# Seven-product down projection for a seventh unit, norms and statistics re-dealt between VectorE and ScalarE, weight sums packed, and a new order table

## The chip, the cores and the metric

The kernel runs on one core of one Trainium2 chip. The time is device microseconds of one launch; less is better. A run's time is that of its slowest core, which is here the only one.

## The reference, cut to what matters

All tensors are bf16. A sequence of 2048 tokens with 512 features goes through two layers; each layer is a long convolution block (A) and a gated feed-forward block (B), with a layer norm without weights ahead of each, and a residual add behind each:

```python
def _A_ref(q, k, v, shift_k, ssm_k, ssm_D):
    # k_shift: k convolved with 4 taps per feature
    kv = k_shift * v
    # y: causal convolution of kv with ssm_k, length 2048, by rfft of length 4096
    y = y + kv * ssm_D[None, None, :]
    return q * y

def _B_ref(x, w_gate, w_up, w_down):          # 512 x 1792, 512 x 1792, 1792 x 512
    g = _silu(x @ w_gate)
    u = x @ w_up
    return (g * u) @ w_down

x = A_q
x = x + _A_ref(_layernorm(x), A_k, A_v, A_shift_k, A_ssm_k, A_ssm_D)
x = x + _B_ref(_layernorm(x), B_w_gate, B_w_up, B_w_down)
# and the same two lines once more
```

The convolution's result y is the same in both layers (its inputs are k, v and the filters), so the kernel computes it once.

## The kernel before, in words

**Units.** The tokens are cut into four blocks c = 0..3 of 512, and each block into two halves h = 0, 1 of 256. The feed-forward of one half block in one layer is a *unit*, written (layer, c, h): 16 units. They run in the order (0,c,0), (0,c,1), (1,c,0), (1,c,1) for c = 0..3, overlapping at their edges. The convolution of block c is done by spectra (matrix products with sine and cosine tables, products of spectra on VectorE named `t`, `Z`, and an inverse) and runs between the units, up to about 200 us.

**A unit.** VectorE or ScalarE makes the statistics of the rows (`ln_stats`, L932: bn_stats and bn_aggr on VectorE; `ln_stats_act`, L943: sums and squared sums by ScalarE's accumulator), GpSimd makes `rstd` by a power (L923), then the norm `n` is applied by VectorE (`normalise`, L987) or by ScalarE (L982, after VectorE has made a small factor `nmr`, L973 or L976). `prologue` (L1002) multiplies n with y, adds it to the residual `xc`, takes statistics again and makes the second norm `z` in the same two ways. `z` is turned by two transposing DMAs on the SyncE queue (L1017) to `zT`, from which TensorE makes gate and up (L432), tile `pf`. ScalarE empties them (`sg` with silu, `hr` or `ht` as a copy), VectorE multiplies the two, and the down projection follows. For some groups of feature tiles the multiplied tile is first turned by DMAs (L1217, `sg<-hr`).

**Down projection, plain.** 14 feature tiles times two token tiles: 28 matmuls of 128x512 into two banks `pd` (L1298). ScalarE copies the two banks to `dn` (L1343, or L1346 where its accumulator also takes the row sums for the next norm's statistics), and one VectorE add puts them into `xc` (L1350).

**Down projection by seven products.** `seven` (L1078) treats the product as a 2x2 block product: seven block products instead of eight. VectorE makes three sums `cb` per group of feature tiles (L1087, L1089, L1091); five sums of `w_down` are made once (`weight_sums`, L1059). A unit then has 49 matmuls of 128x256 (L1108) into four banks. `add_seven` (L1112) has ScalarE empty four banks to `mt` (L1120) and VectorE add them to `xc` in five operations (L1125 to L1132). Before the change six units do this: (1,2,0), (1,2,1), (0,3,0), (0,3,1), (1,3,0) and, for half its features, (1,3,1).

**What sets the order.** Every operation is recorded in a plan with its engine, and the table `ORDER` gives each recorded operation its place. The instructions of every engine are then issued in that order; each engine takes them one after the other, SyncE its DMAs too. Tiles live in rings of slots (`h`, `k`, `hs`, `dg`, `s8`, ...); a new tile of a ring waits until the old one in its slot has been read. The tables at the top say for each unit which engine does what:

- `ST1`: units whose first statistics ScalarE makes; `ST2`: the same for the second.
- `N_ACT` and `Z_ACT`: units whose norm n and z ScalarE makes.
- `STRASSEN`: units whose down projection goes by seven products, with the number of groups.

Of the kernel before, what the change touches and what calls it, by code (L numbers as in the profile page):

```python
# [1616 lines left out]
```

## Time and profile before

| | |
|---|---|
| median of 3 runs | 338.16 us (337.48 to 338.86) |
| the profiled execution | 339.0 us |
| its span, first to last instruction | 337.2 us |
| TensorE busy | 331.3 us (98%), granted clock 0.999 |
| VectorE busy | 310.0 us (92%) |
| ScalarE busy | 268.4 us (80%) |
| GpSimd busy | 40.3 us (12%) |

The profile is of one execution; its span is 1.8 us shorter than that execution's time. Engines are called PE (TensorE matmul), PEld (its weight loads), DVE (VectorE), ACT (ScalarE), POOL (GpSimd) and SP (SyncE). A row of the timeline reads: start, duration, engine, line, operation, output and inputs, how many; in brackets the idle time before it and what ended that. Records of matmuls and of VectorE operations overlap a little with the next one, so the distance between two starts is what an operation occupies.

### The profile page before, as it was taken

The page shows a single profiled execution, that of the slowest core. Times are in us where ns is not written, and L with a number is a line of the kernel's source. Part 1 is how long each engine was busy: PE and PEld are TensorE (multiplying, and loading weights), DVE is VectorE, ACT ScalarE, POOL GpSimd, SP SyncE. Part 2 cuts the span into 40 slices and gives each one's busy share as a digit, 9 for nine tenths or more (in the row PEclk, how much of TensorE's full clock was granted, in tenths as well). Part 3 has the DMA queues.
Part 4 walks back from the last instruction along what each step waited for, and adds up shares of the span by engine and source line. Part 5 has one row for each costly group of instructions (what it writes and reads, how often), then busy time and mean ns, then how long its engine had stood idle before and what let it go on. Part 6 is the DMA issues. An engine that isn't in the chain of part 4 may idle for free.

```text
span 337.2 us, 6314 instructions
## 1 busy us (share of the span) xinstructions
PE 331.3 (98%) x2321; PEld 210.1 (62%) x2321; DVE 310.0 (92%) x580; ACT 268.4 (80%) x542; POOL 40.3 (12%) x54
## 2 busy tenths in 40 slices
PE   8999999999999999999999999999999999999996
PEld 7765864745344556654545465564656797879994
DVE  7799999997999999799899999999999887989785
ACT  7899999999987665899999883858576765658673
POOL 4000100031001010231100201034000000100000
PEclk9999999999999999999999999999999999999999
DMA  7999703476345467941533595747423320212001
GB/s 249 359 284 363 87 10 68 80 175 138 79 96 94 95 124 157 227 95 13 137 80 64 105 173 131 170 80 133 101 50 62 64 50 31 50 32 53 13 2 62
DMA packets 77449, 37.37 MB, mean 111 GB/s; under 512 B 67685, under 2 KB 73706, under 8 KB 77418
## 3 DMA queue, kind: packets, MB, share of 16 engines
q1 hardware_dynamic: 75632, 30.61, 39.6%
q0 software_dynamic: 1632, 6.29, 9.9%
q8 instruction: 18, 0.29, 0.4%
q14 instruction: 13, 0.11, 0.1%
q10 hardware_dynamic: 154, 0.07, 0.1%
HBM read 12.33 MB, written 2.10 MB: 43 GB/s over the span
## 4 chain that ended last, share of the span: by engine, by line
PE 74%; DVE 13%; DMA 7%; ACT 2%; issue 2%; SPq 1%; POOL 0%; DVEq 0%
PE pf L432 40%; PE pd L1298 13%; PE ps L1108 9%; PE ps L432 5%; PE pf L1182 4%; DVE t L774 3%; DMA Z<-t 3%; PE ps L580 2%; DMA kn<-in_A_k_dram 2%; DVE ka L730 1%; DMA kc<-ka 1%; DVE bst L937 1%; DVE hr L1215 1%; SPq L734 1%; DMA zT<-z 1%
## 5 line engine op out<-in xcount | busy, mean ns | idle before, releaser
L432 PEld LDWEIGHTS <-zT 128*128 128x128 bf16 x496 | 48.3, 98 | 55.9 <-DMA zT<-z 2.0
L432 PE MATMUL pf<-wu_sb,zT 128*128 128x512 bf16 x248 | 61.4, 379 | 0.6 <-DMA zT<-z 0.6
L432 PE MATMUL pf<-wg_sb,zT 128*128 128x512 bf16 x248 | 61.2, 379 | 0.0
L432 PE MATMUL pf<-zT,wg_sb 128*128 128x256 bf16 x400 | 49.2, 273 | 0.0
L1208 ACT ACTIVATE sg<-pf 128x512 bf16<-128x512 f32 x62 | 37.5, 617 | 8.6 <-PE pf L432 7.3
L432 PEld LDWEIGHTS <-wg_sb 128*128 128x128 bf16 x400 | 39.0, 98 | 7.3
L1298 PE MATMUL pd<-wd_sb,sg 128*128 128x512 bf16 x176 | 42.4, 379 | 0.0
L1209 ACT CAST hr<-pf 128x512 bf16<-128x512 f32 x62 | 36.6, 601 | 6.0 <-PE pf L432 5.3
L774 DVE TENSOR_TENSOR t<-X,G 128x4096 bf16<-128x4096 bf16 x18 | 41.0, 2283 | 0.0
L1269 ACT ACTIVATE sg<-pf 128x512 bf16<-128x512 f32 x50 | 29.8, 611 | 11.1 <-PE pf L432 9.2
L923 POOL TENSOR_TENSOR rstd<-mv,nhalf 128x2 f32<-128x2 f32 x21 | 18.2, 866 | 142.2 <-DVE mv L938 142.0
L432 PE MATMUL pf<-zT,wu_sb 128*128 128x256 bf16 x272 | 34.6, 273 | 0.1
L432 PEld LDWEIGHTS <-wu_sb 128*128 128x128 bf16 x272 | 26.4, 98 | 6.1 <-issue 0.7
L1298 PEld LDWEIGHTS <-sg 128*128 128x128 bf16 x176 | 17.1, 98 | 19.4 <-DMA sg<-hr 0.6
L1298 PE MATMUL pd<-wd_sb,ht 128*128 128x512 bf16 (+1 forms) x122 | 28.3, 369 | 0.0
L937 DVE BATCH_NORM_STATS2 bst<-xc 128x6 f32<-128x512 bf16 x42 | 27.6, 682 | 0.4
L1273 ACT CAST ht<-pf 128x512 bf16<-128x512 f32 x34 | 20.1, 603 | 5.7 <-PE pf L432 4.3
L541 ACT ACTIVATE X<-ps 128x512 bf16<-128x512 f32 x32 | 19.3, 619 | 3.1 <-PE ps L580 1.3
L1108 PEld LDWEIGHTS <-cb 128*128 128x128 bf16 x195 | 18.7, 98 | 2.8
L1298 PEld LDWEIGHTS <-ht 128*128 128x128 bf16 x122 | 11.9, 98 | 12.9
L1120 ACT CAST mt<-ps 128x512 bf16<-128x512 f32 (+1 forms) x24 | 12.5, 540 | 9.0 <-PE ps L1108 8.8
L1278 DVE TENSOR_TENSOR ht<-ht,sg 128x1024 bf16<-128x1024 bf16 (+1 forms) x33 | 18.3, 557 | 1.4 <-ACT sg L1269 1.1
(157 smaller groups left out, 595.6 us busy)
## 6 DMA issues: line engine op xcount, KB each, us to landing
Z<-t POOLq DMA_DIRECT2D x6, 1024.0 KB, 9.0
hn<-in_A_ssm_k_dram SPq DMA_DIRECT2D x4, 512.0 KB, 4.0
vt<-in_A_v_dram SPq DMA_DIRECT2D x4, 512.0 KB, 6.2
xc<-in_A_q_dram SPq DMA_DIRECT2D x4, 512.0 KB, 5.6
out_dram<-xc SPq DMA_DIRECT2D x15, 128.0 KB, 1.9
wg_sb<-in_B_w_gate_dram SPq DMA_DIRECT2D x1, 1792.0 KB
wu_sb<-in_B_w_up_dram SPq DMA_DIRECT2D x1, 1792.0 KB, 7.6
wd_sb<-in_B_w_down_dram SPq DMA_DIRECT2D x1, 1280.0 KB, 12.3
```

Of the source, the lines that this page charges most:

```text
L432: nc.tensor.matmul(o, lhsT=lhsT, rhs=rhs, start=(n == 0), stop=(n == len(terms) - 1))
L541: add("ACT", act(D), lambda: nc.scalar.activation(out=view(), in_=ps.t[:], func=ACT.Copy, scale=scale), r=[ps], w=[(buf, keys)], conv=conv)
L774: dve(8 * D, lambda t=t, part=part: nc.vector.tensor_mul(out=t.t[:], in0=x.t[:, :, part:part + 1, :].to_broadcast((P, R, 2, D)), in1=g.t[: ...
L923: add("POOL", cost, lambda: nc.gpsimd.tensor_tensor(out=rstd.t[:], in0=var(), in1=nhalf.t[:].to_broadcast((P, n)), op=ALU.pow), r=reads + ...
L937: add("DVE", 0.6, lambda st=st, i=i: nc.vector.bn_stats(out=st.t[:, 0:6], in_=xs[c].t[:, i, :]), r=[(xs[c], (i,))], w=[st])
L1108: nc.tensor.matmul(bank.t[:, half_ * C:(half_ + 1) * C], lhsT=lhsT(i), rhs=rhs(i), start=(first and i == 0 and half_ == 0), stop=(last and ...
L1208: add("ACT", act(D), lambda ps=ps, dst=dst, o=o, which=which: nc.scalar.activation(out=rows(dst, o), in_=ps.t[:], func=ACT.Silu) if which ...
L1209: out=rows(dst, o), in_=ps.t[:], func=ACT.Silu) if which == "g" else nc.scalar.copy(out=rows(dst, o), in_=ps.t[:]),
L1269: add("ACT", act(D), lambda ps=ps, o=o, sg=sg: nc.scalar.activation(out=sg.t[:, o:o + 2, :], in_=ps.t[:], func=ACT.Silu), r=[ps], w=[(sg, ...
L1273: add("ACT", act(D), lambda ps=ps, o=o, ht=ht: nc.scalar.copy(out=ht.t[:, o:o + 2, :], in_=ps.t[:]), r=[ps], w=[(ht, (o // 2,))], due=(uni ...
L1278: dve(n * W, lambda sg=sg, ht=ht: nc.vector.tensor_mul(out=ht.t[:], in0=ht.t[:], in1=sg.t[:]), [sg], [ht], due=(unit, k / pairs, 0.0, "h"))
L1298: nc.tensor.matmul((pds[o] if not cs.start else pds[HP]).t[:, cs], lhsT=ht.tiles(q, o), rhs=wt["d"].t[:, ft, cs], start=(ft == std0 and no ...
```

## The change

1. `STRASSEN` gains (0,2,1), with all four groups: its down projection goes by seven products. The weight sums, which are made ahead of the first such unit, are so recorded one unit earlier.
2. The weight sums `4` and `7`, so far in the slots of rings `k` and `s8`, share one `s8` slot (tile `wst`); the others stay. There are still five.
3. `ST1`, `ST2`, `N_ACT` and `Z_ACT` are new sets. (0,0,0) and (0,0,1) had their first statistics and norm on ScalarE by an argument, and have them now by the sets. In effect first statistics of (1,1,0) and (1,2,1) go to VectorE; n of (0,2,1), (1,1,1) and (1,3,1) goes to VectorE and n of (0,3,1) to ScalarE; z of (1,1,0) goes to VectorE, and z of (0,1,0), (0,1,1), (0,2,1), (0,3,0), (1,2,0), (1,2,1) and (1,3,0) to ScalarE, and the second statistics of (0,0,0), which were never taken that way, leave the set.
4. `ORDER` is a new table. `SUPER` is empty, so the new helpers `mode`, `cond`, `stats_of` and `norms` record either the VectorE or the ScalarE form, as before.

Instructions by engine: TensorE gets 21 matmuls more (28 of 512 columns go, 49 of 256 come). VectorE gets 18 more: four bn_stats, four bn_aggr, twelve `cb` sums, four for adding up, less eight norms, with small ones. ScalarE gets four more: twelve z and four emptied banks, less four n, four squared sums and their like. SyncE's DMAs keep their number.

```diff
+SUPER = ()
-ST1 = lambda l, c, h: (l, c, h) in {(0, 0, 0), (0, 1, 0), (0, 2, 0), (0, 3, 0), (1, 0, 0), (1, 1, 0), (1, 1, 1), (1, 2, 0), (1, 2, 1)}
-ST2 = lambda l, c, h: (l, c, h) in {(0, 0, 0), (0, 2, 1)}
+ST1 = lambda l, c, h: (l, c, h) in {(0, 0, 0), (0, 0, 1), (0, 1, 0), (0, 2, 0), (0, 3, 0), (1, 0, 0), (1, 1, 1), (1, 2, 0)}
+ST2 = lambda l, c, h: (l, c, h) in {(0, 2, 1)}
...
-Z_ACT = lambda l, c, h: (l, c, h) in {(0, 0, 1), (0, 2, 0), (1, 0, 0), (1, 1, 0), (1, 1, 1)}
-N_ACT = lambda l, c, h: (l, c, h) in {(0, 0, 1), (0, 2, 1), (0, 3, 0), (1, 0, 0), (1, 1, 1), (1, 3, 1)}
+Z_ACT = lambda l, c, h: (l, c, h) in {(0, 0, 1), (0, 1, 0), (0, 1, 1), (0, 2, 0), (0, 2, 1), (0, 3, 0), (1, 0, 0), (1, 1, 1), (1, 2, 0), (1, 2, 1), (1, 3, 0)}
+N_ACT = lambda l, c, h: (l, c, h) in {(0, 0, 0), (0, 0, 1), (0, 3, 0), (0, 3, 1), (1, 0, 0)}
...
-STRASSEN={(1,2,0):4,(1,2,1):4,(0,3,0):4,(0,3,1):4,(1,3,0):4,(1,3,1):2}
+STRASSEN={(0,2,1):4,(1,2,0):4,(1,2,1):4,(0,3,0):4,(0,3,1):4,(1,3,0):4,(1,3,1):2}
...
-        a0, a1 = (new(ring, "wsa", [P, NF // 2, C]) for ring in ("h", "k"))
+        a0 = new("h", "wsa", [P, NF // 2, C])
         b = new("hs", "wsb", [P, NF // 2, C])
-        c0, c1 = (new(ring, "wsc", [P, NF // 2, C]) for ring in ("dg", "s8"))
-        ws.update({"1": a0, "4": a1, "3": b, "6": c0, "7": c1})
+        c0 = new("dg", "wsc", [P, NF // 2, C])
+        two = new("s8", "wst", [P, 2, NF // 2, C], parts=2)
+        ws.update({"1": (a0, 0), "4": (two, 0), "3": (b, 0), "6": (c0, 0), "7": (two, 1)})
...
+    def stats_of(kind, unit, c, rows, now, after=(), key_=None):
+        m = mode(kind, unit, now)
...
+    def norms(kind, unit, c, rows, st, now, dsts, due=None):
+        m = mode(kind, unit, now)
```

The new order at three places. In the rows below `m<-Z` and `Z<-m` are steps of the inverse of block 1's convolution, `z` is the second norm that feeds the next unit, `hr` and `ht` are multiplied gate and up tiles.

First TensorE near the start, where the first unit's z is turned by TensorE (`ptz`). Before:

```order
L432 LDWEIGHTS kTb
L432 MATMUL ps<-dg,kTb 128x128
L1045 LDWEIGHTS z
L1045 MATMUL ptz<-ident,z 128x128
```

and now:

```order
L437 LDWEIGHTS kTb
L437 MATMUL ps<-dg,kTb 128x128
L437 LDWEIGHTS fwd
L437 MATMUL ps<-vt,fwd 128x512
L1089 LDWEIGHTS z
L1089 MATMUL ptz<-ident,z 128x128
```

One product of the convolution (`ps<-vt,fwd`) has moved ahead of the turns; two of them still stand between the turns and the unit's first matmul, as before.

Second VectorE where the inverse of block 1 meets the norm z of unit (1,0,1). Before:

```order
L662 TENSOR_TENSOR m<-Z 128x2048 x2
L987 TENSOR_SCALAR z<-xc,mv,rstd 128x512
L987 TENSOR_SCALAR n<-xc,mv,rstd 128x512
L668 TENSOR_TENSOR Z<-m 128x1024
L987 TENSOR_SCALAR z<-xc,mv,rstd 128x512
L679 TENSOR_TENSOR Z<-m 128x2x512 x2
L1215 TENSOR_TENSOR hr<-hr,sg 128x1024
L1212 TENSOR_TENSOR hr<-hr,sg 128x512
L668 TENSOR_TENSOR Z<-m 128x1024
```

and now:

```order
L667 TENSOR_TENSOR m<-Z 128x2048
L1009 TENSOR_SCALAR z<-xc,mv,rstd 128x512 x2
L667 TENSOR_TENSOR m<-Z 128x2048
L684 TENSOR_TENSOR Z<-m 128x2x512
L673 TENSOR_TENSOR Z<-m 128x1024
L1264 TENSOR_TENSOR hr<-hr,sg 128x512
L684 TENSOR_TENSOR Z<-m 128x2x512
```

Both z stand now directly behind the first `m<-Z`, ahead of the second; n has left this stretch, and the last `Z<-m` stands further back.

Third VectorE around the residual add (`xc<-xc,dn`) of unit (0,2,0), with which the work for unit (1,2,0) starts. Before:

```order
L679 TENSOR_TENSOR X_2511<-m 128x2x512 x2
L1350 TENSOR_TENSOR xc<-xc,dn 128x1024
L668 TENSOR_TENSOR X_2511<-m 128x1024
L957 SCALAR_TENSOR_TENSOR nm<-sm,mv 128x2
L774 TENSOR_TENSOR t_2728<-X_2511,G_257 128x4096
L937 BN_STATS bst<-xc 128x6
L987 TENSOR_SCALAR n<-xc,nm,rstd 128x512 x2
```

and now:

```order
L953 BN_STATS bst<-xc 128x6
L673 TENSOR_TENSOR X_2452<-m 128x1024
L954 BN_AGGR mv<-bst 128x2
L1117 TENSOR_TENSOR wst<-wd_sb 128x1792 x2
L1406 TENSOR_TENSOR xc<-xc,dn 128x1024
L976 SCALAR_TENSOR_TENSOR nm<-sm,mv 128x2
L779 TENSOR_TENSOR t_2743<-X_2452,G_242 128x4096
L953 BN_STATS bst<-xc 128x6
L1009 TENSOR_SCALAR n<-xc,nm,rstd 128x512 x2
```

The two packed weight sums stand now ahead of the add; before, four of the five weight sums stood later, the first of them 19 rows behind this add. `cb` sums of unit (0,2,1) follow behind. On TensorE the first matmuls of unit (1,2,0) now stand behind the 80 gate and up matmuls of (0,2,1) and 28 of its 49 products; before they stood behind the whole of (0,2,1), its 28 plain matmuls included.

More of the change, by code (lines that the diff above doesn't have):

```diff
@@ L1 @@
-from contextlib import ExitStack
+from contextlib import ExitStack, nullcontext
 import math
@@ L158 @@
 class Op:
-    __slots__ = ("eng", "cost", "lat", "emit", "bufs", "preds", "succs", "due", "fixed", "conv", "grp", "dest", "sl", "end", "start", "n", "two", "late", "count")
+    __slots__ = ("eng", "cost", "lat", "emit", "bufs", "preds", "succs", "due", "fixed", "conv", "grp", "dest", "sl", "end", "start", "n", "two", "late", "count", "cond", "xc")
 class Plan:
@@ L169, in __init__ @@
         self.ops, self.spans, self.grp = [], [], 0
+        self.cond = None
         self.rings = rings
@@ L174, in buf @@
         b = Buf(ring, name, make, parts)
+        b.cond = self.cond
         self.queue.setdefault(ring, []).append(b)
@@ L179, in add @@
         o = Op()
+        o.cond, o.xc = self.cond, None
         o.eng, o.cost, o.emit, o.conv, o.n = eng, cost, emit, conv, len(self.ops)
@@ L917, in inverse_half, with cond, mode @@
         evacuate_y(k, range(1, R))
+    from contextlib import contextmanager
+    @contextmanager
+    def cond(kind, unit, side):
+        plan.cond = ((kind,) + tuple(unit), side)
+        yield
+        plan.cond = None
+    def mode(kind, unit, now):
+        return "B" if SUPER and (kind in SUPER) else ("A" if now else "D")
     def power(var, reads, n, cost):
@@ L946, in ln_stats_act @@
         sm, prev = sums.pop(key_, (None, None))
+        prevs = prev
+        if prevs is not None:
+            prev = prevs[-1]
         nm = new("mv", "nm", [P, n], F32)
@@ L969, in shift_of @@
     def shift_of(st, n, due=None):
-        mean, rstd = st
+        rd = [b for s in st for b in s]
+        mean, rstd = st[0]
         nmr = new("ve", "nmr", [P, n], F32, parts=n)
@@ L973, in shift_of @@
             add("DVE", 0.08, lambda: nc.vector.scalar_tensor_tensor(out=nmr.t[:], in0=mean.t[:, :, 0], scalar=-1.0, in1=rstd.t[:],
-                                                                    op0=ALU.mult, op1=ALU.mult), r=[mean, rstd], w=[nmr], due=due)
+                                                                    op0=ALU.mult, op1=ALU.mult), r=rd, w=[nmr], due=due)
         else:
-            add("DVE", 0.08, lambda: nc.vector.tensor_mul(out=nmr.t[:], in0=mean.t[:], in1=rstd.t[:]), r=[mean, rstd], w=[nmr], due=due)
+            add("DVE", 0.08, lambda: nc.vector.tensor_mul(out=nmr.t[:], in0=mean.t[:], in1=rstd.t[:]), r=rd, w=[nmr], due=due)
         return nmr
     def normalise(dst, dkeys, view, c, i, o, st, nmr=None):
-        mean, rstd = st
+        rd = [b for s in st for b in s]
+        rs = [s[1] for s in st]
+        mean, rstd = st[0]
         if nmr is not None:
@@ L983, in normalise @@
                                                             scale=rstd.t[:, o:o + 1], bias=nmr.t[:, o:o + 1]),
-                r=[(xs[c], (i,)), (nmr, (o,)), rstd], w=[(dst, dkeys)])
+                r=[(xs[c], (i,)), (nmr, (o,))] + rs, w=[(dst, dkeys)])
             return
@@ L1010, in prologue @@
             dve(HP * D, lambda: nc.vector.tensor_add(out=x.t[:, sl, :], in0=x.t[:, sl, :], in1=n.t[:]), [n], [(x, rows)])
-            st = ln_stats_act(c, rows) if ST2(layer, c, h) else ln_stats(c, rows)
-            means[c, h] = st[0]
-            nmr = shift_of(st, HP) if Z_ACT(layer, c, h) else None
-            for o, i in enumerate(rows):
-                z = new("z", "z", [P, D])
-                normalise(z, (0,), lambda z=z: z.t[:], c, i, o, st, nmr)
+            unit = (layer, c, h)
+            st = stats_of("S2", unit, c, rows, ST2(layer, c, h))
+            means[c, h] = [s[0] for s in st]
+            zz = [new("z", "z", [P, D]) for _ in rows]
+            norms("Z", unit, c, rows, st, Z_ACT(layer, c, h), [(z, (0,), lambda z=z: z.t[:]) for z in zz])
+            for (o, i), z in zip(enumerate(rows), zz):
                 add("SP", 1.29, lambda z=z, o=o: nc.sync.dma_start_transpose(
@@ L1033, in prologue @@
                 [(n, (o,))], [(x, (i,))])
-        st = ln_stats(c, rows)
-        means[c, h] = st[0]
+        st = [ln_stats(c, rows)]
+        means[c, h] = [st[0][0]]
         stats = plan.ops[-2]
@@ L1337, in ffn @@
             sm = None
-            if layer == 0 and ST1(1, c, h):
-                sm = new("st", "sm", [P, 2 * HP], F32, parts=2 * HP)
+            s1 = mode("S1", (1, c, h), ST1(1, c, h))
+            if layer == 0 and s1 in "AB":
+                with (cond("S1", (1, c, h), "A") if s1 == "B" else nullcontext()):
+                    sm = new("st", "sm", [P, 2 * HP], F32, parts=2 * HP)
                 sums[1, c, h] = sm, means.pop((c, h))
@@ L1345, in ffn @@
                 else:
-                    add("ACT", act(D) + 0.14, lambda o=o: nc.scalar.activation(
+                    ev_ = add("ACT", act(D) + 0.14, lambda o=o: nc.scalar.activation(
                         out=dn.t[:, o, :], in_=pds[o].t[:], func=ACT.Copy, accum_out=sm.t[:, o:o + 1]), r=[pds[o]], w=[(dn, (o,)), (sm, (o,))],
                         due=(unit, 1.0, 3.0, "h"))
+                    if s1 == "B":
+                        ev_.cost, ev_.xc = act(D), (("S1", 1, c, h), "A", 0.14)
             sl = span(rows)
@@ L1476 @@
     shift_mul(0, "pf", False, due=-49)
[L1477 removed]
+    normed[0, 0, 0] = apply_norm(0, 0, due=-47)
     if SUMS:
@@ L1532 @@
         evacuate_y(0, (1, 3))
-    normed[0, 0, 1] = apply_norm(0, 1, on_act=True, after=first)
+    normed[0, 0, 1] = apply_norm(0, 1, after=first)
     prologue(0, 0, 1)
```

62 lines of the change are left out of this document (41 added, 21 removed), and 149 rows, old and new, of the table ORDER.

## The prediction

> **What bounds the kernel now.** I read the page first, then the chain of waits, then TensorE's timeline where the chain leaves it. The page, instructions behind the x:
>
> ```profile
> span 337.2 us, 6314 instructions
> PE 331.3 (98%) x2321; PEld 210.1 (62%) x2321; DVE 310.0 (92%) x580; ACT 268.4 (80%) x542; POOL 40.3 (12%) x54
> ```
>
> TensorE is nearly always busy, VectorE not far behind. The chain that ended last, in order of time (start, us, what):
>
> ```profile
> 122.21 1.04 PE pf L432 x4
> ...
> 146.01 6.04 PE pd L1298 x28
> ...
> 210.01 12.15 PE pf L432 x80
> 222.16 6.04 PE pd L1298 x28
> ...
> 277.56 5.35 PE ps L1108 x49
> ...
> 332.67 1.32 PE pd L1298 x12
> ```
>
> From 122.21 to 334.0 us the chain lies on TensorE alone: every matmul taken away there is time taken from the end, as long as nothing else comes late. Before 122 us the chain runs mostly through VectorE, GpSimd and DMAs, and TensorE waited in three places (in brackets the idle time ahead of the row):
>
> ```profile
> 31.73 0.72 PE L1045 MATMUL ptz<-ident,z 128*128 128x128 bf16 x8 [0.21 <-DVE z L987]
> ...
> 33.15 1.03 PE L432 MATMUL pf<-zT,wu_sb 128*128 128x256 bf16 x8
> ...
> 86.03 0.88 PE L432 MATMUL ps<-Z,inv 128*128 128x512 bf16 x3
> 87.13 0.38 PE L432 MATMUL ps<-Z,inv 128*128 128x512 bf16 x1 [0.23 <-DVE Z L679]
> 87.89 1.47 PE L432 MATMUL pf<-wu_sb,zT 128*128 128x512 bf16 x6 [0.38 <-DMA zT<-z]
> ...
> 122.21 1.04 PE L432 MATMUL pf<-wu_sb,zT 128*128 128x512 bf16 x4 [0.22 <-DMA zT<-z]
> ```
>
> Matmul records end about 0.16 us late (a matmul of 512 columns is shown with 0.38 us but occupies 6.04/28 = 0.216), so a wait is that much longer than its bracket. At 86 to 88: four `ps<-Z,inv` from 86.03 should have ended at 86.89, the next started at 87.89, so 1.0 us is lost. At 122.21: 0.22 + 0.16 = 0.39. Around 31.73 about 0.37.
>
> **Part one: the seventh unit.** Unit (0,2,1) is the row at 222.16: 28 plain matmuls, 6.04 us. Seven products are 49 matmuls of 256 columns; the row at 277.56, of (0,3,0), gives 5.35 us for 49. The saving is 6.04 - 5.35 = **0.69 us**, on the chain. The Trainium skill's page "TensorE: Matmul & The Clock Gate", section Back-to-back issue gap, speaks against this: it gives about 131 ns for a sustained matmul of 512 columns, by which 28 take 3.7 us and the edit would lose 1.7 us. The rows show 216 ns, so that gets no chance here.
>
> **Part two: what the other engines get.** Mean durations, by groups (xcount | busy, mean ns):
>
> ```profile
> L937 DVE BATCH_NORM_STATS2 bst<-xc 128x6 f32<-128x512 bf16 x42 | 27.6, 682 | 0.4
> L938 DVE BATCH_NORM_AGGREGATE mv<-bst 128x2 f32<-128x9 f32 x42 | 6.5, 181 | 0.3
> L987 DVE TENSOR_SCALAR z<-xc,mv,rstd 128x512 bf16<-128x512 bf16 x20 | 7.7, 408 | 0.3 <-POOL rstd L923 0.3
> L1087 DVE TENSOR_TENSOR cb<-sg 128x512 bf16<-128x512 bf16 x9 | 3.8, 419 | 0.1
> L1091 DVE TENSOR_TENSOR cb<-sg 128x256 bf16<-128x256 bf16 x9 | 2.6, 285 | 0.1
> L982 ACT ACTIVATE z<-xc,nmr,rstd 128x512 bf16<-128x512 bf16 x10 | 8.6, 870 | 0.0
> L961 ACT ACTIVATE jk<-xc,nm 128x512 bf16<-128x512 bf16 x22 | 15.8, 717 | 0.2
> L1120 ACT CAST mt<-ps 128x512 bf16<-128x512 f32 (+1 forms) x24 | 12.5, 540 | 9.0 <-PE ps L1108 8.8
> ```
>
> VectorE: 4 x (0.68 + 0.18) of statistics, 6 x 0.42 + 5 x 0.29 + 0.2 of `cb` sums and 4 x 0.42 for the adding up are added, 8 x 0.41 of norms go: 3.4 + 4.2 + 1.7 - 3.3 = +6.0 us, with the records' overlap of 0.08 each taken out (below) nearer +4.5. ScalarE: 12 z at 0.87 and 4 banks at 0.54 are added, 4 n (taken like z) and 4 squared sums at 0.72 go: 10.4 + 2.2 - 3.5 - 2.9 = at most +6.2 us, less the accumulator reads that go with the sums, against 337.2 - 268.4 = 69 us idle. None of this is on the chain after 122 us as long as VectorE and ScalarE stay ahead; if they don't, each us late is a us on the end. GpSimd has as many `rstd` (two more behind bn_aggr, two fewer behind `ve`), and SyncE as many DMAs. The packing leaves five sums; its one possible price, a slot of `s8` held for longer, lies between 0 and one postponed product, 2.2 us; I take 0, since no row shows a wait for a slot there.
>
> **Part three: the new order.** (a) The start. One `ps<-vt,fwd` now stands in the gap ahead of the turns, where 0.37 us are lost. The unit's first matmul at 33.15 still waits for the same copies, with 0.22 us more done: **-0.21**.
>
> (b) At 86 us. VectorE and SyncE there:
>
> ```profile
> 81.94 2.36 DVE L662 TENSOR_TENSOR m<-Z 128x2048 bf16<-128x2048 bf16 x2 [1.52 <-DMA Z<-t]
> 84.22 0.41 DVE L987 TENSOR_SCALAR z<-xc,mv,rstd 128x512 bf16<-128x512 bf16 x1
> ...
> 84.65 2.50 SPq L1017 DMA_TRANSPOSE zT<-z  x2
> ```
>
> The queue issued zT as soon as z was there, 84.65, and the unit's first matmul followed at 87.89, so it landed at about 87.85. Now the first z stands one `m<-Z` (1.14 us) earlier, so zT lands at about 86.7. But the `Z<-m` steps stand behind two `m<-Z` and both z: from 81.94 that is 2 x 1.14 + 2 x 0.33 us, then 0.6 for each step and 0.34 for the multiplication ahead of the third. They end at 85.5, 86.1 and 87.0, so the first inverse matmuls wait some 0.7 us from 85.4 to 86.1, then four `pd` (0.86), two inverse matmuls (0.43), and the unit starts at about 87.8, with 0.43 us more matmul work behind it than before, of which 0.21 is (a)'s. With the rounding that is **-0.28**; the ends are -1.0 (all of the wait) and +0.4 (the steps later still).
>
> (c) At 122 us. z of (0,1,1) was VectorE's, behind two products; ScalarE makes it now, and its DMAs stand further ahead of the unit. That wait goes: **-0.39**, at worst it stays.
>
> (d) What comes late next. VectorE between the residual adds of (0,1,0) and (0,2,0):
>
> ```profile
> 127.00:165.00 38.00, 38.00 (x221) 21.50 (x220) 34.26 (x59) 32.41 (x72) 7.75 (x8) 1.00 0.61 129
> 165.00:211.00 46.00, 46.00 (x247) 23.87 (x245) 44.59 (x55) 38.30 (x76) 3.32 (x3) 1.00 0.55 110
> ...
> DVE n L987 <- POOL rstd L923: 1.2, 1, 1.2
> DVE nmr L973 <- POOL rstd L923: 0.9, 1, 0.9
> DVE xc L1350 <- ACT dn L1346: 0.7, 1, 0.7
> DVE hr L1215 <- ACT sg L1208: 0.6, 1, 0.6
> DVE ka L730 <- ACT kc L726: 0.6, 1, 0.6
> DVE n L1009 <- ACT n L982: 0.4, 1, 0.4
> ```
>
> The fourth figure of a window is VectorE's busy time: it idled 3.7 + 1.4 = 5.1 us, of which the six named waits (127 to 211 us) are 4.4. The new order has 4.5 us more VectorE work in this stretch: two more weight sums of 1.0, two bn_stats, four n, two z for two others, one `X<-m`, less two `wu`. TensorE's order stays, so those waits have to shrink. Two of them (1.2 and 0.4) wait for norms and statistics of (1,1,0) and (1,1,1) that leave ScalarE, and the 0.7 now has statistics ahead of the add. The others wait for ScalarE, and one (0.9) for GpSimd; ScalarE here loses two squared sums, two z and four n and gets two z: 1.4 + 1.7 + 3.5 - 1.7 = 4.9 us less. I take it that VectorE comes to the add of (0,2,0) in time.
>
> (e) Behind that add. The rows from there:
>
> ```profile
> 210.96 0.69 DVE L1350 TENSOR_TENSOR xc<-xc,dn 128x1024 bf16<-128x1024 bf16 x1
> ...
> 211.57 0.69 DVE L668 TENSOR_TENSOR X<-m 128x1024 bf16<-128x1024 bf16 x1
> ...
> 220.27 2.25 DVE L774 TENSOR_TENSOR t<-X,G 128x4096 bf16<-128x4096 bf16 x1
> 222.56 1.22 DVE L778 TENSOR_TENSOR t<-t,t 128x2048 bf16<-128x2048 bf16 x1
> ...
> 227.57 1.08 DVE L1072 TENSOR_TENSOR wsa<-wd_sb 128x1792 bf16<-128x1792 bf16 x1
> ...
> 220.50 2.57 POOL L923 TENSOR_TENSOR rstd<-mv,nhalf 128x2 f32<-128x2 f32 x1 [5.07 <-DVE mv L938]
> ...
> L923 POOL TENSOR_TENSOR rstd<-mv,nhalf 128x2 f32<-128x2 f32 x21 | 18.2, 866 | 142.2 <-DVE mv L938 142.0
> ```
>
> The add's record is 0.69 us, and the next operation starts 0.61 behind it: an operation occupies its record less 0.08. From this add to the last `cb` sum of (0,2,1) VectorE now has two products (2.2 each), two combinations (1.14), six operations of 1024 (0.60), eight of 512 (0.34), two n (0.33), five of 256 (0.2), three bn_stats (0.65), a weight sum (1.0) and small ones: 17.9 us, from 0.95 us behind the down projection of (0,2,0) (it ended at 210.01, the add started at 210.96). TensorE comes to the last products after 12.15 (row at 210.01), eight matmuls of (1,2,0) at 0.216 and 42 products at 0.109: 18.5 us. So VectorE is late by 18.85 - 18.45 = 0.4. And `rstd`, 0.87 us in the mean, took 2.57 from 220.50: it ended at 223.07, 0.55 behind the product that VectorE ran beside it (220.27 + 2.25). In the new order the factor `nmr` for z of (1,2,0) stands right behind such a product, so VectorE waits 0.55; queued behind `nmr` are the `cb` sums, for which TensorE waits in its products, and ScalarE's z. The Trainium skill, page "GPSIMD Engine Reference", section Key points, says that GpSimd shares its memory interfaces with VectorE and contends with its two-input operations; this row agrees. Together **+0.95**; the ends are 0 and, with the waits of (d) left, 4.5 more. z of (1,2,0), its DMAs and zT come about as late, and hide in the same wait.
>
> **The sum.** -0.69 - 0.21 - 0.28 - 0.39 + 0.95 = -0.62. The profiled execution of 339.0 us would take 338.4; it stands 0.84 above the median of the runs, so from 338.16 the forecast is **337.5 us**. Half a per cent, 1.7 us, is about what a measurement of this kernel can tell from no change.
>
> **Rivals.**
> - *All waits go and none comes.* VectorE keeps up everywhere: -0.69 - 0.21 - 1.0 - 0.39 = -2.3, 335.9 us. For it: after 122 us TensorE never waits in the profile before. Against: VectorE gets 5 us more.
> - *VectorE becomes the bound* (slower). If none of the 4.4 us of waits in (d) shrinks, the add of (0,2,0) comes 4.5 us late, z of (1,2,0) with it, and TensorE waits for it, because 3 us of other matmul work that stood ahead of that unit are gone: -0.62 + 4.5 = +3.9, 342.1 us. It decides from 2.3 us of lateness, where the sum passes +1.7. For it: 5.1 us idle against 4.5 us of new work. Against: ScalarE's relief in the same stretch.
> - *Half of that,* and the change brings nothing: 2.2 us late, +1.6, 339.8 us; the seventh unit's gain is spent on a wait for zT.
>
> **Chances.** Forecast (336.5 to 338.8) 0.45; all waits gone 0.25; half late 0.17; VectorE the bound 0.13. The range leaves out the last and reaches from 335.6, a little past the second, to 339.9. Faster by over 0.5% (under 336.5): 0.26, the second and a sliver. Slower by over 0.5% (over 339.85): 0.19, the last and a third of the half. Between: 0.55.
>
> **What would show it.** Right: 49 `ps` matmuls in (0,2,1) at 0.109 us each; no wait for zT near 122 us; one of about 0.5 to 1 us in (0,2,1)'s products or at the first matmuls of (1,2,0), near 226 us. Wrong: VectorE idle of over 3 us between 127 and 211 us, with TensorE waiting for zT of (1,1,1) or (1,2,0); or waits in the units behind 240 us, where I expect none.

## The result and the profile after

The changed kernel takes 347.37 us in the median of 4 runs (344.72 to 348.43), the kernel before 338.1; the ratio is 1.0261, 95% interval 1.02 to 1.0323. It is slower by 9 us, where I had forecast 337.5 and a range to 339.9. The profiled execution took 347.14 us. The head of its page:

```profile
span 345.4 us, 6357 instructions
...
PE 331.6 (96%) x2312; PEld 211.9 (61%) x2342; DVE 313.2 (91%) x598; ACT 271.9 (79%) x538; POOL 43.7 (13%) x54
```

The span grew by 345.4 - 337.2 = 8.2 us, while TensorE's busy time hardly moved: its idle time grew from 5.9 to 13.8 us. The waits of TensorE in order of size (total, times, longest, in us) name most of it:

```profile
PE pd L1350 <- DMA sg<-hr: 4.3, 1, 4.3
PE ps L437 <- DVE vt L743: 1.6, 1, 1.6
PE ps L1160 <- DMA sg<-hr: 0.8, 1, 0.8
...
PE pf L437 <- ACT ht L1325: 0.5, 1, 0.5
PE pf L437 <- ACT sg L1321: 0.4, 1, 0.4
```

The two largest stand side by side. TensorE's timeline there, in units (1,1,0) and (1,1,1):

```profile
188.33 0.85 PE L437 MATMUL ps<-vt,fwd 128*128 128x512 bf16 x2 [1.64 <-DVE vt L743]
193.43 1.49 PE L1350 MATMUL pd<-wd_sb,sg 128*128 128x512 bf16 x3 [4.25 <-DMA sg<-hr]
```

and what the other engines do meanwhile (GpSimd, SyncE's queue, VectorE, then the chain that ended last):

```profile
178.39 5.09 POOL L939 TENSOR_TENSOR rstd<-ve,nhalf 128x2 f32<-128x2 f32 x1 [14.96 <-ACT ve L984]
183.44 1.22 POOL L787 DMA_DIRECT2D Z<-t  x1
```

```profile
178.41 6.45 SPq L739 DMA_TRANSPOSE kc<-ka  x4
184.96 11.38 SPq L1269 DMA_TRANSPOSE sg<-hr  x6
```

```profile
182.25 0.68 DVE L1267 TENSOR_TENSOR hr<-hr,sg 128x1024 bf16<-128x1024 bf16 x1
183.50 0.69 DVE L743 TENSOR_TENSOR vt<-kc,vt 128x1024 bf16<-128x1024 bf16 x1 [0.56 <-DMA kc<-ka]
...
187.58 0.69 DVE L743 TENSOR_TENSOR vt<-kc,vt 128x1024 bf16<-128x1024 bf16 x1 [1.65 <-DMA kc<-ka]
```

```profile
184.96 8.02 DMA sg<-hr
192.98 0.45 issue
193.43 1.49 PE pd L1350 x3
```

Read together: GpSimd issues the large accumulating DMA `Z<-t` (1 MB) at 183.44. In this stretch it takes 9.0 us to land, until about 192.4. A transpose of `sg<-hr` issued at 184.96 lands 8.02 us later, at 192.98; the two behind it, issued at 187.1 and 190.2, land 6.4 and 3.7 us after their issue, all three within 1.6 us of the large one's end. So it reads for these three transposes in the changed kernel, and for the transposes of 176 to 197 us in the kernel before:

```profile
DMA to landing us min/median/max: 3.7/6.4/8.0
```

```profile
DMA to landing us min/median/max: 2.4/2.4/7.3
```

SyncE's queue also needs 2.1 to 3.0 us to issue each of the three, where 1.2 is usual.

The packets show what holds the transposes. Of the DMA queues, q0 carries the accumulating DMA and q1 SyncE's transfers (packets, MB, share of the 16 DMA engines). From 189.5 to 191.5 us, while the large DMA is under way, and then q1 from 191.5 to 193.5:

```profile
q0 software_dynamic: 79, 0.31, 98.5%
q1 hardware_dynamic: 79, 0.02, 7.3%
```

```profile
q1 hardware_dynamic: 1553, 0.37, 101.7%
```

The two queues take turns packet by packet, 79 against 79, but a packet of the accumulating DMA has some 4 KB and one of a transpose some 0.25 KB, so that the transposes move at about a sixteenth of its rate until it is through. The same count is 82 against 82 from 190 to 192 us in the run below that lets the DMA out early in the kernel before. Why the transposes move no packet at all from 187.5 to 189.5, and why their issue takes longer, stays open.

The last `kc<-ka`, issued at 183.60, lands after 3.9 us, and that is the wait of 1.64 us: `vt` of 187.58 needs it. In the kernel before, the same accumulating DMA went out 8 us later, behind the issue of the last `kc<-ka` and of all but two of the `sg<-hr` transposes of this stretch, because GpSimd had an `rstd` in front of it that waited for ScalarE:

```profile
190.66 0.95 POOL L923 TENSOR_TENSOR rstd<-ve,nhalf 128x2 f32<-128x2 f32 x1 [26.29 <-ACT ve L965]
191.56 1.22 POOL L782 DMA_DIRECT2D Z<-t  x1
```

Behind the wait the clock falls. The columns are TensorE's busy time and count, PEld, VectorE, ScalarE, GpSimd, then the granted clock, the DMA share and GB/s:

```profile
189.00:193.40 4.40, 0.18 (x1) 0.13 (x2) 4.33 (x7) 1.22 (x3) 0.00 (x0) 0.58 1.05 179
193.40:197.00 3.60, 3.57 (x11) 1.49 (x11) 0.00 (x0) 1.19 (x2) 0.00 (x0) 0.56 0.57 111
```

TensorE works from 193.4 to 197 at 0.56 of its clock, which costs 3.6 x 0.44 = 1.6 us more. VectorE has nothing to do in that second stretch: it is the engine that waits, not the one that is waited for.

A smaller pair of waits stands at 138 to 142 us. TensorE and then ScalarE:

```profile
139.33 1.02 PE L437 MATMUL pf<-wu_sb,zT 128*128 128x512 bf16 x4 [0.43 <-ACT sg L1321]
140.82 1.03 PE L437 MATMUL pf<-zT,wu_sb 128*128 128x256 bf16 x8 [0.47 <-ACT ht L1325]
```

```profile
135.55 0.63 ACT L971 ACTIVATE jk<-xc 128x512 bf16<-128x512 bf16 x1 [2.90 <-DMA xc<-in_A_q_dram]
...
137.98 0.72 ACT L980 ACTIVATE jk<-xc,nm 128x512 bf16<-128x512 bf16 x1
138.59 0.20 ACT L980 ACTIVATION_READ_ACCUMULATOR jk<-xc,nm 128x1 f32 x1
138.68 0.59 ACT L1321 ACTIVATE sg<-pf 128x512 bf16<-128x512 f32 x1
```

ScalarE waits for the load of token block 2 and has its statistics (`jk`) queued ahead of the evacuations `sg` and `ht` for which TensorE waits.

With the 0.16 us that a matmul's record overlaps, the new waits are 4.41 + 1.80 at 186 to 193, 0.59 + 0.63 at 138 to 142, 1.0 at 231 (the 0.8 above, in the seventh unit's products) and 0.4 near 271; with 1.6 of clock they make 10.4. The seventh unit gives back 0.69 and the old waits at 86 and 122 us 1.4. That makes +8.3, against 8.2 measured. That the two agree to 0.1 is luck: TensorE's wait for an input load in the first 7 us, a fourth place that the prediction left out, was 0.7 us in the profile before and has no row in the one after; it was 1.0 and 0.2 in two of the runs below.

### The profile page after: what moved, and what is told of

Its sections match the earlier page's. It is cut to its first block, busy times and chain, and to the rows that moved or that the text cites. A ratio compares the mean times of both kernels' runs of the same rounds, so it can differ in the third digit from the quotient of the medians.

```text
span 345.4 us, 6357 instructions
## 1 busy us (share of the span) xinstructions
PE 331.6 (96%) x2312; PEld 211.9 (61%) x2342; DVE 313.2 (91%) x598; ACT 271.9 (79%) x538; POOL 43.7 (13%) x54
## 4 chain that ended last, share of the span: by engine, by line
PE 41%; DVE 37%; DMA 11%; ACT 4%; issue 4%; SPq 2%; POOL 1%; DVEq 0%; ACTq 0%; POOLq 0%
PE pf L437 19%; PE ps L1160 9%; PE pd L1350 6%; DVE t L779 6%; DMA sg<-hr 5%; DVE bst L953 4%; DVE m L667 3%; PE ps L437 3%; PE pf L1234 3%; DVE hr L1267 2%; DVE ka L735 2%; DVE Z L783 2%; DMA kc<-ka 2%; DMA out_dram<-xc 2%; DVE n L1053 2%
## 5 line engine op out<-in xcount | busy, mean ns | idle before, releaser
L437 PE MATMUL pf<-wu_sb,zT 128*128 128x512 bf16 x243 | 60.4, 379 | 0.7 <-ACT sg L1321 0.4
L437 PE MATMUL pf<-wg_sb,zT 128*128 128x512 bf16 x236 | 60.2, 379 | 0.6
L1350 PE MATMUL pd<-wd_sb,sg 128*128 128x512 bf16 x154 | 39.2, 389 | 4.6 <-DMA sg<-hr 4.3
L939 POOL TENSOR_TENSOR rstd<-mv,nhalf 128x2 f32<-128x2 f32 x23 | 20.2, 878 | 139.9 <-DVE mv L954 129.3
L953 DVE BATCH_NORM_STATS2 bst<-xc 128x6 f32<-128x512 bf16 x46 | 30.1, 683 | 0.3
L1350 PEld LDWEIGHTS <-sg 128*128 128x128 bf16 x160 | 15.8, 100 | 23.4 <-DMA sg<-hr 5.1
L1350 PE MATMUL pd<-wd_sb,ht 128*128 128x512 bf16 (+1 forms) x108 | 25.0, 367 | 0.1
L1160 PEld LDWEIGHTS <-cb 128*128 128x128 bf16 x230 | 22.3, 98 | 3.7 <-DVE cb L1141 0.3
L1172 ACT CAST mt<-ps 128x512 bf16<-128x512 f32 (+1 forms) x28 | 14.6, 534 | 8.0 <-PE ps L1160 7.6
L1267 DVE TENSOR_TENSOR hr<-hr,sg 128x1024 bf16<-128x1024 bf16 x25 | 17.1, 682 | 3.4 <-ACT sg L1260 2.7
```

The costliest lines, as they stand in the source:

```text
L437: nc.tensor.matmul(o, lhsT=lhsT, rhs=rhs, start=(n == 0), stop=(n == len(terms) - 1))
L939: add("POOL", cost, lambda: nc.gpsimd.tensor_tensor(out=rstd.t[:], in0=var(), in1=nhalf.t[:].to_broadcast((P, n)), op=ALU.pow), r=reads + ...
L953: add("DVE", 0.6, lambda st=st, i=i: nc.vector.bn_stats(out=st.t[:, 0:6], in_=xs[c].t[:, i, :]), r=[(xs[c], (i,))], w=[st])
L1160: nc.tensor.matmul(bank.t[:, half_ * C:(half_ + 1) * C], lhsT=lhsT(i), rhs=rhs(i), start=(first and i == 0 and half_ == 0), stop=(last and ...
L1267: dve(n * W, lambda: nc.vector.tensor_mul(out=hr.t[:], in0=hr.t[:], in1=sg.t[:]), [sg], [hr], due=(unit, k / pairs, 0.0, "h"))
L1350: nc.tensor.matmul((pds[o] if not cs.start else pds[HP]).t[:, cs], lhsT=ht.tiles(q, o), rhs=wt["d"].t[:, ft, cs], start=(ft == std0 and no ...
```

## The experiments

The theory (A): transposes that SyncE issues while the accumulating DMA is under way land only when it is through, or nearly; the new order lets it out just ahead of the last `kc<-ka` and three `sg<-hr` (the expectations, written from a coarser reading, speak of eight). Rivals: VectorE is late (B), or ScalarE's new share makes the convolution's transposes late (C). Every kernel was timed beside the kernel before; ratios are to it.

**One `rstd` later.** On ScalarE (on VectorE the `nmr` that reads this `rstd` also goes behind one `G<-H`):

```diff
 L980 ACTIVATE jk,sm<-xc,nm 128x512 x2
-L984 ACTIVATE ve<-sm,eps 128x2
 L1261 CAST hr<-pf 128x512
...
 L546 ACTIVATE X<-ps 128x512 x3
+L984 ACTIVATE ve<-sm,eps 128x2
```

> The changed kernel with one `rstd` and the tiny ScalarE instruction that feeds it (`ve`) made later, as late as in the kernel before: GpSimd's large accumulating DMA `Z<-t`, which stands right behind that `rstd`, is then issued at about 191 us in place of 183.44; no work is added or taken away. Theory A (transposes that SyncE issues behind that DMA land only when it is through): the eight transposes that landed at about 193 us land 2.4 to 2.7 us after their issue, TensorE's waits of 1.8 us at 186 and 4.3 us at 189 mostly go, and so do the matmuls at half the clock behind them: 338.5 to 341 us. Rival B (VectorE is late, as the prediction's rival had it) and rival C (ScalarE's new share makes the shift convolution's products late): the work of both engines is as before, so 346 to 348 us.

344.35 us, ratio 1.0181 (1.0159 to 1.0204): 3 of 9 us back, fewer than expected. TensorE's waits and GpSimd's rows say why:

```profile
PE pf L437 <- DMA zT<-z: 2.3, 1, 2.3
PE pd L1350 <- DMA sg<-hr: 2.1, 2, 1.3
```

```profile
194.44 1.22 POOL L787 DMA_DIRECT2D Z<-t  x1
207.86 1.20 POOL L787 DMA_DIRECT2D Z<-t  x1 [12.20 <-DVE t L783]
```

The waits of 186 to 193 shrank from 6.2 to 0.5 us, and the granted clock stayed at 1.00: A's mechanism. But new ones of 0.9, 1.5 and 2.5 us came at 204 to 212. The last is the same trap at its next place: the accumulating DMA of 207.86 goes out just ahead of a transpose of zT issued at 208.20, which lands 6.6 us later. Before, the stall had hidden this.

**The sum by VectorE instead of the DMA.**

```diff
-Z_DMA = lambda i, j: True
+Z_DMA = lambda i, j: (i, j) != (2, 1)
```

> The changed kernel with the one accumulating DMA `Z<-t` of 183.44 us taken away; VectorE makes this sum by one addition of 128x4096 (about 2.2 us) instead. Theory A: the waits at 186 to 193 us go with the DMA, and VectorE's 2.2 us cost between nothing and their full length: 339 to 342 us. Rival B (VectorE late): 2.2 us more on the engine that is late, 348 to 350 us. Rival C: no change, 346 to 348 us.

342.75 us, 1.0136 (1.0119 to 1.0152). B would have it slower; it is 4.6 us faster than the changed kernel, with 2.2 us more on VectorE.

**The same DMA earlier in the kernel before.** On GpSimd:

```diff
+L782 DMA Z<-t_2254 128x2x2048
 L923 TENSOR_TENSOR rstd<-ve,nhalf 128x2
-L782 DMA Z<-t_2254 128x2x2048
```

> The kernel before with two instructions of GpSimd's queue exchanged: the same `Z<-t` ahead of the `rstd` that holds it until 191.56 us, so that it goes out when its sum is ready, at about 185.3 us. Theory A: the transposes issued between 185.4 and 193 us now land at about 194.5 us, the last of the shift convolution's among them, and TensorE waits: 341 to 345 us in place of 338.1. Rivals B and C: nothing is added to VectorE or ScalarE, 337.5 to 338.7 us.

344.45 us, 1.0185 (1.0158 to 1.0212): two instructions exchanged make the kernel before 6.2 us slower. GpSimd's and TensorE's rows:

```profile
184.40 1.22 POOL L782 DMA_DIRECT2D Z<-t  x1 [21.45 <-DVE t L778]
```

```profile
194.47 3.37 PE L1298 MATMUL pd<-wd_sb,sg 128*128 128x512 bf16 x8 [4.52 <-DMA sg<-hr]
```

The same wait, on the same tile, at the same place, and eight matmuls take 3.37 us (1.89 at the full clock). Neither VectorE nor ScalarE has anything new here, so B and C are out as causes of the stall.

**Statistics behind the evacuations.** On ScalarE (two of the moves):

```diff
-L980 ACTIVATE jk,sm<-xc,nm 128x512
 L1321 ACTIVATE sg<-pf 128x512
-L980 ACTIVATE jk,sm<-xc,nm 128x512
-L984 ACTIVATE ve<-sm,eps 128x2
 L1325 CAST ht<-pf 128x512
+L980 ACTIVATE jk,sm<-xc,nm 128x512
```

> The changed kernel with the five ScalarE instructions of the first statistics of (0,2,0), which wait for the token block's load at 135.55 us, each put behind the evacuations that TensorE waits for (same work, other order on ScalarE alone). If these statistics are what holds the evacuations back, TensorE's waits of 0.6, 0.64 and 0.1 us between 138 and 142 us go; behind 180 us theory A lets the stall stand, unless the earlier start changes which of VectorE's gaps lets the accumulating DMA out: 345.5 to 347 us, or 339 to 341 with the stall gone. If the load alone is the cause, or a later wait takes the gain: 347 to 348 us.

347.0 us, 1.0261 (1.0229 to 1.0294). The two waits at 138 to 142 are gone from TensorE's timeline; 0.3 came at 143 and 0.5 at 146 (`pd<-wd_sb,sg`, for a transpose). The stall starts 0.7 us earlier than in the changed kernel and is as long, but the clock behind it stays at 0.50 until 197.0 in place of 196.5 us, so that at 201 us TensorE is only 0.04 us ahead. The total did not move beyond its spread, so these runs price the two waits at nothing that can be told from zero.

**VectorE without the gap at 183.5 us.** The `rstd` of 178.39 ended at 183.48, in VectorE's idle 0.56 us. On VectorE:

```diff
-L743 TENSOR_TENSOR vt<-kc,vt 128x1024
 L667 TENSOR_TENSOR m<-H 128x2048
 L1267 TENSOR_TENSOR hr<-hr,sg 128x1024
 L743 TENSOR_TENSOR vt<-kc,vt 128x1024
 L1117 TENSOR_TENSOR wsb<-wd_sb 128x1792
+L743 TENSOR_TENSOR vt<-kc,vt 128x1024
```

> The changed kernel with two instructions of VectorE's queue put further back, no work added or taken away: the first `vt<-kc,vt` behind the `m<-H` and the `hr<-hr,sg` that followed it, the second behind the weight sum `wsb`. In the changed kernel VectorE waits 0.56 us for that first `vt` (its transpose is late), and at the end of this wait the `rstd` that GpSimd had held since 178.39 is through, and the accumulating DMA behind it goes out at 183.44. Theory A with this gap as its trigger: VectorE has no gap there any more, `rstd` is held until 186 us or later, and the DMA goes out behind most of the transposes: 340 to 344 us. If the gap isn't the trigger (the `rstd` goes through by itself, or ScalarE sets it), the DMA goes out at 183 to 184 as before: 346.5 to 348.5 us.

347.56 us, 1.0269 (1.0254 to 1.0285): no gain. GpSimd and VectorE:

```profile
178.61 6.23 POOL L939 TENSOR_TENSOR rstd<-ve,nhalf 128x2 f32<-128x2 f32 x1 [14.95 <-ACT ve L984]
184.80 1.22 POOL L787 DMA_DIRECT2D Z<-t  x1
```

```profile
184.55 0.69 DVE L1267 TENSOR_TENSOR hr<-hr,sg 128x1024 bf16<-128x1024 bf16 x1 [0.25 <-ACT sg L1260]
```

The gap at 183.5 went, and `rstd` ended 1.4 us later, at 184.84, 0.29 us behind the end of VectorE's next gap; the DMA went out at 184.80, which is still ahead of three transposes. So the order on VectorE moves the issue, but that a gap sets it is not shown: in the run without the DMA (below) the same `rstd` took 5.10 us and ended at 182.64, where VectorE has no gap (`vt` from 182.06, `m<-H` from 182.67).

**Without that DMA, and with half of it.** First without:

```diff
-            add("POOL", 1.3, lambda: nc.gpsimd.dma_start(out=z.t[:], in_=t1.t[:], ...
+            add("POOL", 1.3, (lambda: None) if (i, j) == (2, 1) else lambda: ...
```

> The changed kernel without the accumulating DMA of 183.44 us, and without anything in its place: this term is left out of the sum Z. Against the run in which VectorE made that sum (342.75 us) it takes 2.2 us from VectorE between 190 and 205 us and nothing else. If VectorE is what TensorE waits for at 205 and 208 us (waits of 1.5 and 0.6 us, and no gap on VectorE over 0.4 us from 187 to 218): 340.4 to 341.4 us, these waits mostly gone. If VectorE is not late there: 342.3 to 343.2 us.

340.72 us, 1.0061 (1.0042 to 1.0081). No wait of 186 to 193 us is left, and none over 0.3 us of 204 to 212. But I had read the run with VectorE's addition wrongly: its addition stood right ahead of the `hr` whose transpose TensorE waited for, so the 1.5 and 0.6 us there were made by the addition. Without it, VectorE's rows and TensorE's:

```profile
199.71 0.68 DVE L1267 TENSOR_TENSOR hr<-hr,sg 128x1024 bf16<-128x1024 bf16 x1
```

```profile
202.75 1.89 PE L1350 MATMUL pd<-wd_sb,sg 128*128 128x512 bf16 x8
204.47 1.46 PE L1350 MATMUL pd<-wd_sb,ht 128*128 128x512 bf16 x6
```

No wait: VectorE comes in time here, but with so little to spare that 2.2 us more cost nearly their whole length (342.75 against 340.72). The profiled execution is the fastest of the five, 339.35 us; its waits over 0.4 us are 0.45 and 0.64 at 138 to 140, 1.0 at 224 and 0.5 at 264. What makes the others up to 1.8 us longer no trace shows.

With half of it:

> The changed kernel with the accumulating DMA of 183.44 us over the first half of its elements only (0.5 MB in place of 1 MB; the other half of this term is left out). Theory A in the form that transposes wait until that transfer's bytes are through: they land at about 188 in place of 193 us, TensorE's wait of 4.3 us falls under 0.7 us and its clock isn't halved behind it: 340.5 to 342.5 us. If it is the DMA's issue or its queue and not its size that holds the transposes: 346 to 348 us.

```diff
-nc.gpsimd.dma_start(out=z.t[:], in_=t1.t[:], accum_op=ALU.add, ...
+nc.gpsimd.dma_start(out=z.t[:, 0:2], in_=t1.t[:, 0:2], accum_op=ALU.add, ...
```

345.83 us, 1.0215 (1.0196 to 1.0234), outside what I expected. The half transfer (its last figure is the time to landing), and TensorE behind it:

```profile
Z<-t POOLq DMA_DIRECT2D x1, 512.0 KB, 5.7
```

```profile
190.26 0.85 PE L437 MATMUL ps<-vt,fwd 128*128 128x512 bf16 x2 [3.58 <-DVE vt L743]
190.95 1.43 PE L1350 MATMUL pd<-wd_sb,sg 128*128 128x512 bf16 x4
...
192.60 1.91 PE L1350 MATMUL pd<-wd_sb,sg 128*128 128x512 bf16 x4
```

It lands at 183.42 + 5.7 = 189.1, and the transpose issued at 184.8 lands 4.9 us later, at 189.7: size does set how long the `sg` transposes are held. But the last `kc<-ka`, issued at 183.45, right behind the DMA, was held until about 189.5 (in the changed kernel it landed at 187.5), so `vt` and TensorE wait 3.6 us where they had waited 1.6. The 4.25 us wait is gone; the trap caught another.

**Orders alone.** Three edits: the late `rstd`, the later statistics, and the second `t<-t,t` of 206 us behind two weight sums, so that the DMA of 207.86 goes out later.

```diff
-L783 TENSOR_TENSOR t<-t,t 128x4x512
 L684 TENSOR_TENSOR X<-m 128x2x512
...
 L1117 TENSOR_TENSOR wst<-wd_sb 128x1792 x2
+L783 TENSOR_TENSOR t<-t,t 128x4x512
```

> The changed kernel with three edits of order and no work added: the late `rstd` of the first experiment (344.35 us alone), the later first statistics of (0,2,0), and the second half of the combination `t<-t,t` of 206.3 us put behind two weight sums on VectorE, so that the accumulating DMA that follows it at 207.86 goes out behind the two transposes of zT it held up there (TensorE waited 2.5 us for them at 212). Theory A: these 2.5 us go, and the 1.3 us of waits at 138 to 142: 340 to 342 us. If VectorE is the bound of the stretch from 140 to 218 us, so that a wait taken away comes back as VectorE's: 342.5 to 344.5 us.

341.79 us, 1.0086 (1.0063 to 1.011), as theory A had it: 5.6 of the 9 us are back. What is left stands again in SyncE's queue:

```profile
191.99 8.32 SPq L1414 DMA_DIRECT2D out_dram<-xc  x4
201.03 1.27 SPq L1269 DMA_TRANSPOSE sg<-hr  x1
204.71 0.34 SPq L513 DMA_DIRECT2D xc<-in_A_q_dram  x1
```

The accumulating DMA now goes out at 193.90 and lands 8.2 us later. An output DMA issued beside it takes 5.6 us in place of 1.9, the transpose of 201.03 lands after 4.1 us, and the next waits behind a load that waits for an output DMA.

**Two further attempts.** On SyncE the second transpose goes ahead of that load, on VectorE one `hr` ahead of a statistic; in the second kernel `ve` is also one step earlier.

```diff
-L1269 DMA_TRANSPOSE sg<-hr 128x4x128
+L1269 DMA_TRANSPOSE sg<-hr 128x4x128 x2
 L513 DMA xc<-in_A_q_dram 128x2048
```

> The changed kernel with the three edits of the run before (341.79 us) and two more, again of order alone: on SyncE the second of the two transposes of the `hr` of 200.3 us goes ahead of the token block's load, which waits there until 204.7 for an output DMA; on VectorE the second `hr<-hr,sg` of the seven-product unit goes ahead of one of the statistics in front of it. Theory A and the bookkeeping by waits: TensorE's wait of 1.3 us at 208 goes, and 0.4 to 0.8 of the 1.1 us at 225: 339.7 to 340.4 us. If VectorE's lateness comes back in other places: 341.2 to 342 us.

> As the other run of this call, with the late `ve` and `rstd` about 1 to 2 us earlier than there, so that the accumulating DMA goes out at 192 to 193 in place of 193.9 us and is through before the transpose issued at 201 lands. Theory A: TensorE's wait of 0.95 us at 204 shrinks by 0.4 to 0.9 us as well: 339 to 340 us. If the DMA then holds the last transposes issued before it, or VectorE alone sets that wait: within 0.4 us of the other run, or slower by up to 3 us.

341.78 us (1.0101, 1.0077 to 1.0126) and 341.84 (1.0106, 1.0078 to 1.0134): nothing gained. In the first, the wait aimed at, 1.3 us at 208, is gone, but 0.4 were added at 204, 0.8 came at 215 and 0.4 at 224. In the second the DMA is through at 201.75, the transpose issued at 202.12 lands in 2.8 us and TensorE's wait at 204 is gone, as theory A had it; but 1.6 us came at 216, for an evacuation by ScalarE.

**The sum itself later.**

```diff
-L783 TENSOR_TENSOR t<-t,t 128x4x512
 L1267 TENSOR_TENSOR hr<-hr,sg 128x1024
+L667 TENSOR_TENSOR m<-H 128x2048
...
 L1267 TENSOR_TENSOR hr<-hr,sg 128x1024
+L1196 TENSOR_TENSOR wu<-wu_sb 128x512 x2
...
+L783 TENSOR_TENSOR t<-t,t 128x4x512
```

> The changed kernel with edits of order alone, in another way than the late `rstd`: here `rstd` goes out early as in the changed kernel, and the second half of the combination `t<-t,t`, which ended at 182.3 us there, is put behind a step of H's inverse at about 190 us, so that the accumulating DMA behind it goes out at 191 to 192 us, when no transpose is issued for 9 us, and is through at 200. In VectorE's place at 181 to 186 us stand `m<-H` and two `wu` sums that stood elsewhere. The other edits of the two runs before (341.8 us) stay, the second `t<-t,t` of 205 us goes a little further back, behind the residual add and its `nm`, and one n of ScalarE goes behind an evacuation. Theory A: the transposes issued at 201 to 203 us land in 2.4 us in place of 4.5, TensorE's waits of 1.4 us at 204 and of 0.8 at 214 go, none comes at 186 to 193: 339.2 to 340.4 us. If VectorE has no room left for the moved work: 341.3 to 343 us.

> As the other run of this call, with that combination one step of H's inverse earlier on VectorE, so that the accumulating DMA goes out some 0.6 us earlier. Theory A: if it goes out ahead of the last transpose of 191 us, that one lands at 200 (TensorE then waits up to 3 us for it); if not, within 0.4 us of the other run.

346.77 us (1.0257, 1.0225 to 1.0288) and 347.23 (1.0242, 1.021 to 1.0274): both missed, by a fault of the edit. VectorE's row:

```profile
185.85 1.23 DVE L667 TENSOR_TENSOR m<-H 128x2048 bf16<-128x2048 bf16 x1 [3.85 <-DMA kc<-ka]
```

The row shows `m` waiting 3.85 us for the transposes of `ka`. As I read it, the sum that ends later holds its slot of ring `s8` longer, and `m` takes the slot of `ka` instead; no run tries this by itself. The accumulating DMA went out at 196.17, when no transpose was under way, and the next, of 206.31, landed in 2.4 us, which fits theory A but could not show in the time.

None of these versions beats the kernel before, and the two parts of the change were not timed one without the other.

## Why the prediction was wrong

**The step that failed** is in part two: "GpSimd has as many `rstd` (...), and SyncE as many DMAs." I counted them and did not place them. The second statistics of unit (0,2,1) have their `rstd` behind ScalarE's `ve` in both kernels, but ScalarE makes `ve` 12 us earlier in the new order (178 in place of 190.6), and the accumulating DMA queued behind that `rstd` moves with it: from 191.56 to 183.44, ahead of the transposes that VectorE and TensorE need next instead of behind them. By the waits that is worth 4.41 + 1.80 + 1.6 = 7.8 of the 8.2 us; by the runs 6.7 us, what the changed kernel gains without this DMA, and 6.2, what the kernel before loses when it goes out early. It was there to be seen: the row at 190.66 has 26.29 us of idle time ending with `ve`, and the transpose issued at 192 in the kernel before took 7.3 us to land where the others took 2.4, at no cost only because nobody waited for it.

The Trainium skill's page "DMA: Bandwidth & Descriptors", section Issuing engines are not separate DMA queues, says that DMAs issued by different engines run on the same 16 DMA engines and interleave. The trace agrees: SyncE's queue is no protection from GpSimd's (a share of 1.05 in the window from 189), and the packets of the two alternate, 79 against 79. But a fair turn by packets is none by bytes: the transpose took 8.0 us in place of 2.4, nearly the rest of the large one.

**The seventh unit** saves what was forecast per matmul. Two rows of the changed kernel, eight products from one start to the next:

```profile
232.63 1.04 PE L1160 MATMUL ps<-wd_sb,cb 128*128 128x256 bf16 x8
233.50 1.03 PE L437 MATMUL pf<-wg_sb,zT 128*128 128x512 bf16 x3
```

0.87 / 8 = 0.109 us. But its products waited 1.0 us for a transpose of `sg`, a wait at the place and of the size of (e)'s +0.95, so that the term of -0.69 was right and this unit alone gave nothing back in any of the runs that kept 1.0 us there.

**(a)** gave nothing: the product that was to fill the gap at 31 us now waits 0.37 us itself, for ScalarE. **(b)** gave all of its 1.0 us, the end of the range and not the -0.28 taken, and **(c)** its 0.39. Together -1.4 where I had -0.88.

**(d)** held. VectorE, the third busy figure, is nearly without a gap from 140 to 180 us, and comes in time, as the run without the DMA showed at 200:

```profile
140.00:180.00 40.00, 39.30 (x202) 19.92 (x205) 39.65 (x65) 38.02 (x77) 8.03 (x8) 1.00 0.44 85
```

The rival "VectorE becomes the bound" gave the number nearest to the result, 342.1, for a reason that the runs refuted. But its "in time" has no slack, which may be why the orders tried could not bring the rest back. Over the whole span VectorE is busy 3.2 us longer than before (I had 4.5 to 6.0) and ScalarE 3.5 (at most 6.2), with four instructions fewer on ScalarE, 538, and not four more: my count left out the accumulator reads that went.

**(e)** came true in place and size: 1.0 us at 231, in the products of (0,2,1), for 0.95 forecast. The cause is in part another: TensorE waits for a transpose of `sg`, issued behind an `hr` that VectorE started at 226.29, and not for `cb` sums. With that `hr` earlier (the five orders) the wait halves, and 0.4 us for `cb` comes ahead of it. The 1.2 us at 138 to 142, by statistics on ScalarE ahead of evacuations, stand in no term of the prediction.

What stays open: whether an order exists that has no transpose under way beside any accumulating DMA and still keeps VectorE in time, and whether a plain DMA of the same size would hold the transposes as an accumulating one does. If all the new waits went, the sum of the terms above would be -0.69 - 1.4 = -2.1 us, an estimate.

## What to carry to other kernels

Count a change's DMAs by when they go out and what else is under way then, not by how many there are: here a large accumulating DMA on one queue held small transposes on another until it was nearly through. Ask of each such DMA what stands ahead of it in its queue, since a wait there may be what keeps it out of the way, and a change that removes the wait releases the DMA. When a stall is taken away, look for the next place where the same two meet before trusting the sum.
